# Two transformer layers on one core: a small matrix sent from another engine's DMA queue, and work of the query path, the token sums and the reloads put in other slots

## The chip, the core and the metric

The kernel runs on one core of a Trainium2 chip. The core has a matrix engine (TensorE; PE in the profile, PEld for its weight loads), three elementwise engines (VectorE: DVE, ScalarE: ACT, GpSimd: POOL), and SyncE (SP), which does nothing but issue DMAs. Sixteen DMA engines move data for all queues. The engines run on their own and meet through semaphores. The metric is the time of one execution in microseconds (us) on the device; lower is better.

## What is computed

Two layers over one sequence of 2048 tokens of width 448, in float32. With H = 16 heads of width 28 and F = 1792:

```python
phi = lambda t: jnp.where(t > 0, t + 1, jnp.exp(t)) + 1e-6
def A(x):                                  # linear attention
    q, k, v = split(x @ wqkv)              # (heads, tokens, 28) each
    pq, pk = phi(q), phi(k)
    kv = einsum("bhsd,bhse->bhde", pk, v); z = einsum("bhsd->bhd", pk)
    num = einsum("bhqd,bhde->bhqe", pq, kv)
    den = einsum("bhqd,bhd->bhq", pq, z) + 1e-6
    return (num / den) @ wo
def B(x):                                  # MLP
    return gelu(x @ w1 + b1) @ w2 + b2
for _ in range(2):
    x = x + A(layernorm(x))
    x = x + B(layernorm(x))
```

Each float32 matrix product is made of three passes: both operands are split into a high and a low part of a format that the matrix engine takes at full rate, and high by high, low by high and high by low are added up.

## The kernel before

The tokens stand in 16 tiles of 128, and in four blocks of 512. A layer has these stages. First come keys, values and queries of all tokens and the state of the attention; the queries go to DRAM (`pq_d`). Then a small transition forms from the state and `wo` a matrix M of 448 by 448, split into Mh and Ml, each in four pieces of 112 rows (`trans_ms`). Its use as weights (tiles `wq`) needs 128 rows to a tile, so `trans_chunks` (L916) copies rows between tiles by 14 DMAs, two to a chunk where a border falls inside; all are issued on SP's queue at L925, eight at the start of block 0 and six after the next piece of `mlp1`.

`classic(l, b, tr)` (L1321) then runs blocks 0 and 1 of the MLP, 14 steps each. In step i the matrix engine does `mlp1` of piece i+1 (11 matmuls into `hp`), what `behind` puts in, and `mlp2` of piece i (12 matmuls into four accumulators `y`). Between the two stands ScalarE's gelu (g, L1202) and its high part gh (L1173), and VectorE's low part gl (L1177). `make` prepares the next pair of pieces of w1: loads into `temp` (L420, L421, SP's queue) and casts into W (L425 and L430 on ScalarE, L426 to L432 on GpSimd).

`behind` (L1279) reads one row of the table `PLAN` for each of the 28 steps and does in it the query path of a later token tile, ahead of where the MLP needs it. For tile j of block k: `ld` loads pq (L942), `z` multiplies by the key sum (GpSimd, L952), `p` divides (VectorE: L963, L965, L967, L974) and transposes (L312, L313) into a square `sq`; `sq` stores this to DRAM (L319), and `lq` spreads it over the partitions (four DMAs at L331, tile `sp`); `q` splits that into qh (ScalarE, L365) and ql (VectorE, L366); `o` multiplies by wq (L1022 to L1026, into `op`), adds to x (L1043) and takes the norm's statistics; `n` and `sx`, `lx`, `x` do for the MLP's input what p, sq, lq, q do for the query. `r` and `b` load residuals and add the bias.

Blocks 2 and 3 share most of the MLP's first product by seven products in Strassen's manner: `eight(l, k)` (L1378), k = 0 to 6. Its operands are the four quarters A11, A12, A21, A22 of the tokens and the sums S1 to S4 of them (`token_sum`, L1107) split into high and low (`token_piece`: casts on ScalarE, L1112, subtractions on VectorE, L1113); the words s and t of PLAN make most of them in the last steps of block 1, `PLACES` gives each a slot. The weights of a product are sums of w1's pieces as well (VectorE, L458 to L480). The results of the products (hx, hy, hz) are read by copies and adds (L1146, L1401, L1418, L1423) and go through the gelu. Half of the gelus, those of block 3, go to DRAM (`g_d`), and `rest(l)` (L1454) brings them back (`gb`, loaded by `Came.load`, L1447), splits them and runs block 3's second product (w2 only). In between `rest` starts the next layer: x comes back (`load_to`, L86), is normalized (L528), transposed, stored (`sq_a`, L319), spread (`sp<-sq_a`, L331) and split (ScalarE, XH L365).

What sets the order: each engine runs its instructions in the order in which the program was written; nothing is rescheduled. All DMAs of SP and ScalarE take eight semaphores in turn, so an issue waits, whatever its data, until the DMA eight issues before it has landed. Tiles with one tag rotate through a fixed number of buffers ("e" has five; `gb` is of that tag), and a write into a buffer waits for the last reader of what it held.

Of the kernel before, what the change touches and what calls it, by code (L numbers as in the profile page):

```python
# [22 lines left out]
def linear_attn_mlp_kernel(  # L23
# [21 lines left out]
    G = 112  # L45
    NG = D // G
    NP = NF // 2
# [30 lines left out]
    def f(ap):  # L78
        return ap.bitcast(F32)
# [836 lines left out]
    def trans_chunks(tr):  # L916

        tr.ch = [(piece("q", c), piece("q", 3 + c)) for c in range(3)]
        tr.cr = piece("q", 6)

        def rows(src, out, at, lo, hi):
            r = lo
            while r < hi:
                n = min(hi, (r // G + 1) * G) - r
                sp.dma_start(f(out[at + r - lo:at + r - lo + n]), f(src[r // G][r % G:r % G + n]))  # L925
                r += n

        for c in range(3):
            if c == 2:
                yield  # L930
            rows(tr.Mh, tr.ch[c][0], 0, c * 128, (c + 1) * 128)
            rows(tr.Ml, tr.ch[c][1], 0, c * 128, (c + 1) * 128)
        rows(tr.Mh, tr.cr, 0, TL, D)
        rows(tr.Ml, tr.cr, 64, TL, D)


    pqt, qs, pzs = {}, {}, {}
# [114 lines left out]
    def add_bias(l, b, j):  # L1052
        t = b * 4 + j
        pool.tensor_tensor(xt[l, t], xt[l, t], b2b, op=OP.add)
# [12 lines left out]
    def m_prep(l, b, j):  # L1067
# [1 line left out]
        turn(xns.pop(("m", l, b * 4 + j)), ("m", l, b), j)  # L1069


    PLACES = ({"A11": 0, "S1": 1, "S2": 4, "A12": 5, "S3": 6, "S4": 2, "A22": 3},
              {"A11": 0, "S1": 5, "S2": 4, "A12": 1, "S3": 6, "S4": 2, "A22": 3})
    SUMS = {"S1": ("A21", "A22", OP.add), "S2": ("S1", "A11", OP.subtract),
            "S3": ("A11", "A21", OP.subtract), "S4": ("A12", "S2", OP.subtract)}
# [33 lines left out]
    def token_piece(l, name, h, eng=dve):  # L1109
        x = view(l, name, h)  # L1110
        hi, lo = (cols(placed(l, k, name, h)) for k in range(2))
        act.copy(hi, x)  # L1112
        eng.tensor_tensor(lo, x, f(hi), op=OP.subtract)  # L1113
# [91 lines left out]
    def mlp2(l, b, i, then=lambda: None):  # L1205
        gh, gl = gs.pop(i)
        first, last = i == 0, i == NF - 1
        n = i ^ (b > 1)
        hi, lo = w2h[:, n], w2l[:, n]
        end = l == LAYERS - 1 and b == NB - 1  # L1210
        if first:
            accs[l, b] = [bank("acc", 4, f"y{j}")[:, :D] for j in range(4)]
        acc = accs[l, b]
        for j in range(4):
            t = b * 4 + j
            s = slice(j * 128, (j + 1) * 128)
            if end and j == 3 and last:

                for h, eng in enumerate((act, sp)):
                    n = slice(h * D // 2, (h + 1) * D // 2)  # L1220
                    o = bank("m", 2, "yh")[:, :D // 2]
                    pe.matmul(o, gh[:, s], hi[:, n], start=True, stop=False)
                    pe.matmul(o, gh[:, s], lo[:, n], start=False, stop=False)
                    pe.matmul(o, gl[:, s], hi[:, n], start=False, stop=True)
                    xs = xt[l, t][:, n]
                    dve.tensor_tensor(xs, o, xs, op=OP.add)
                    eng.dma_start(x_d[l + 1][t * 128:(t + 1) * 128, n], xs)
                continue
            stop = last or (end and j == 3 and i == NF - 2)
            pe.matmul(acc[j], gh[:, s], hi, start=first, stop=False)  # L1230
            pe.matmul(acc[j], gh[:, s], lo, start=False, stop=False)  # L1231
            pe.matmul(acc[j], gl[:, s], hi, start=False, stop=stop)  # L1232
            if stop:
                xs = xt.pop((l, t)) if last else xt[l, t]
                dve.tensor_tensor(xs, acc[j], xs, op=OP.add)
                if j == 0:
                    then()
                if last:
                    sp.dma_start(x_d[l + 1][t * 128:(t + 1) * 128, :], xs)
# [7 lines left out]

    PLAN = (
        "p10 z11",
        "p11 sq10 z12 g10",  # L1250
        "p12 z13 lq10 g11",
        "p13 sq11 g12 g13 ld20",
        "q10 lq11 ld21",
        "q11 o10 ld22",
        "q12 o11 n10 ld23 z20",
        "q13 o12 n11 sx10 p20 z21",
        "o13 n12 lx10 p21 z22 sq20",
        "n13 sx11 p22 z23 lq20 g20 g21",
        "x10 lx11 p23 sq21 g22 g23",
        "x11 q20 lq21 ld30 ld31",  # L1260
        "x12 x13 q21 o20 ld32 ld33 z30",
        "q22 o21 n20 p30 z31",
        "q23 o22 n21 sx20 p31 z32 sq30",
        "o23 n22 p32 z33 lq30 g30 g31",
        "n23 sx21 p33 sq31 g32 g33",
        "q30 lq31 lx21 r10 r11",
        "q31 o30 r12 r13",
        "q32 o31 n30 tA111 b10",
        "q33 o32 n31 sx30 lx20 b11",
        "o33 n32 tA121 b12",  # L1270
        "n33 lx30 sx31 tA110 b13",
        "lx31 sS10 tA120",
        "tS10 sS30 sS20",
        "tS20 sS40 sS11 tS11 sS31",
        "tS40 sS21 tS21 sS41",
        "tA220 tA221 tS41",
    )

    def behind(l, i, tr):  # L1279
# [41 lines left out]
    def classic(l, b, tr):  # L1321

        if b == 0:
            mlp1(l, 0, 0)
            moves = trans_chunks(tr)
            next(moves)
        for i in range(NF):
            if i + 1 < NF:
                mlp1(l, b, i + 1)
            elif b == 0:  # L1330
                mlp1(l, 1, 0)
            if b == 0 and i == 0:
                next(moves, None)
            n = first_pair(l, b) + i // 2 + 2
            late = b and i >= NF - 4
            if late:
                if i > NF - 4:
                    make(first_pair(l, 2))
            elif i % 2:
                make(n)  # L1340
            if i % 2 == 0 and (b == 0 or i < NF - 2):
                make(n + 1)
            behind(l, b * NF + i, tr)
            if b == 0 and 9 <= i < 13:
                add_bias(l, 0, i - 9)
            if b == 0 or i < NF - 2:
                mlp2(l, b, i)
            if late:
                make(first_pair(l, 2))
            elif i % 2 == 0:  # L1350
                make(n)
            if b and i == NF - 1:
                make(n)

    def beside(l, k):

        nonlocal st_k, st_q
        if k == 0:
            for tok in "S30 S31".split():
                token_piece(l, tok[:-1], int(tok[-1]))  # L1360
        if 2 <= k < 6:
            back(l, 2, k - 2)
        if 3 <= k < 7:
            add_bias(l, 2, k - 3)
        if l + 1 == LAYERS:
            return
        if k == 6:
            load_to(l + 1, PRE - 1)
        if k == 1:
            st_k = stage_square(wqkv[:, D:2 * D])  # L1370
        if k == 2:
            split_kq("k", st_k)
        if k == 3:
            st_q = stage_square(wqkv[:, :D])
        if k == 4:
            split_kq("q", st_q)

    def eight(l, k):  # L1378

        n = first_pair(l, 2) + k  # L1380
        c = Pair(l, k, n)

        def step():
            if k < NP - 1:
                make(n + 1)

        c.product(1)
        s1 = c.keep(c.X, "s1")
        if k == 0:
            make(n)  # L1390
            beside(l, k)
        step()
        if k == 0:
            mlp2(l, 1, NF - 2)
            c.product(2)
            mlp2(l, 1, NF - 1)
        c.product(5)
        s5 = c.keep(c.Y, "s5")
        step()
        if k == 0:  # L1400
            dve.tensor_tensor(s1, s1, c.Z, op=OP.add)  # L1401
        if k:
            mlp2(l, 2, 2 * k - 1)
        c.product(6)
        s2 = c.keep(c.X, "s2")
        make(n)
        if k < NP - 2:
            make(n + 2)
        step()
        if k == 0:  # L1410
            c.high(s1, 0)
        else:
            c.product(2)
            dve.tensor_tensor(s1, s1, c.Z, op=OP.add)  # L1414
            c.high(s1, 0)
            step()
        c.product(7)
        dve.tensor_tensor(s5, c.X, s5, op=OP.add)  # L1418
        c.low(0)
        c.later(s5, 1)  # L1420
        step()
        c.product(3)
        dve.tensor_tensor(s2, s2, c.Y, op=OP.add)  # L1423
        c.high(s2, 1)
        step()
        c.product(4)
        if k == NP - 1:
            gb.load(l, 2)
        c.low(1)
        c.later(c.X, 0)  # L1430
        step()
        if k:
            beside(l, k)
        mlp2(l, 2, 2 * k)
        step()

    class Came:
# [5 lines left out]

        def load(self, l, n=1):
            for i in range(self.n, min(self.n + n, NF)):
                self.x[i] = t512("e", 5, "gb")
                sp.dma_start(self.x[i], g_d[l, i])  # L1447
            self.n = min(self.n + n, NF)

    gb = Came()  # L1450
# [136 lines left out]
```

## Time and profile before

| | |
|---|---|
| median of 3 runs | 892.22 us (891.28 to 892.72) |
| the profiled execution's own time | 889.03 us |
| its span, first to last instruction | 887.3 us |
| granted clock of the matrix engine, mean | 0.990 |
| matrix engine | 855.7 us busy, 4085 matmuls |
| DMA | 142.95 MB, mean 161 GB/s |

The profile is of one execution, so its stages add up to the span and not to the median; 1.7 us lie outside the span, and the execution is 3.2 us under the median. In rows of the timeline the columns are start, duration, engine, line, operation, output and inputs, and in brackets the idle time of the engine just ahead of the row, with what ended it. In rows of windows, each engine has its busy time and, in brackets, its count; PEclk is the granted clock as a share of full speed. Matmuls overlap: one that takes 0.36 us starts 0.20 us after the one before it, so starts are compared, not durations. Time that the matrix engine is idle is what there is to win; idle time of another engine counts only where the matrix engine waits for it.

### The profile page before, as it was taken

Reading aid. Unit: us, or ns where it says so; the run is one execution under the profiler, and the core shown is the slowest. Engines: PE = TensorE matmul, PEld = TensorE weight load, DVE = VectorE, ACT = ScalarE, POOL = GpSimd, SP = SyncE. Lnnn points to the kernel's source line nnn. Section 1 sums busy time; section 2 is a strip of 40 time slices with the busy share of each in tenths; the row PEclk is TensorE's granted clock in tenths of the full one; section 3 lists DMA queues with packets and bytes.
Section 4 is the critical chain, followed back from the end, with each engine's and each line's share of the span. In section 5 each row is a group of like instructions: output and inputs, shape, how many; then the busy total and the mean of one; then the engine's idle time right before and its main releaser. Section 6 shows DMA issues by size and latency. Waiting matters only on the chain.

```text
span 887.3 us, 12710 instructions
## 1 busy us (share of the span) xinstructions
PE 855.7 (96%) x4085; PEld 757.9 (85%) x4085; DVE 581.2 (65%) x1094; ACT 443.5 (50%) x883; POOL 384.3 (43%) x460
## 2 busy tenths in 40 slices
PE   9999999899999989999899999998999998899998
PEld 8999898688888868887699998987888887788887
DVE  7987686378976664456578876763879657534343
ACT  7667664334344557564345665543252435566531
POOL 3546533345644653650442243042556356444311
PEclk9999999899999999999999999998999999999999
DMA  5476746736576134316835543476375760332172
GB/s 172 139 240 197 197 137 209 224 120 217 202 240 203 48 119 138 126 66 233 235 117 178 183 136 94 145 223 211 129 229 198 241 196 23 118 109 89 48 233 83
DMA packets 105800, 142.95 MB, mean 161 GB/s; under 512 B 12036, under 2 KB 92804, under 8 KB 105732
## 3 DMA queue, kind: packets, MB, share of 16 engines
q1 hardware_dynamic: 104980, 141.72, 50.3%
q8 instruction: 32, 0.52, 0.3%
q10 hardware_dynamic: 752, 0.41, 0.2%
q14 instruction: 36, 0.29, 0.1%
HBM read 88.94 MB, written 49.02 MB: 155 GB/s over the span
## 4 chain that ended last, share of the span: by engine, by line
PE 72%; DMA 10%; DVE 9%; ACT 3%; issue 2%; SPq 2%; POOL 0%; DVEq 0%; ACTq 0%
PE hp L1200 10%; PE G L725 8%; PE psk L383 7%; PE psq L383 7%; PE hx L1142 7%; PE y L1230 7%; PE y L1231 6%; PE y L1232 6%; PE hy L1142 3%; DMA gb<-g_d 2%; DMA sp<-sq_m 2%; DMA sq_q<-sq 1%; DMA sp<-sq_q 1%; PE hz L1142 1%; DMA temp<-in_B_w_dram 1%
## 5 line engine op out<-in xcount | busy, mean ns | idle before, releaser
L1230 PE MATMUL y<-w2h,gh 128*128 128x448 f32 x447 | 164.0, 367 | 4.9 <-ACT gh L1173 3.8
L1231 PE MATMUL y<-w2l,gh 128*128 128x448 f32 x447 | 164.4, 368 | 0.0
L1232 PE MATMUL y<-w2h,gl 128*128 128x448 f32 x447 | 161.9, 362 | 1.3 <-DVE gl L1177 1.0
L1177 DVE TENSOR_TENSOR gl<-g,gh 128x512 fp32r<-128x512 f32 x84 | 64.3, 765 | 107.0 <-ACT gh L1173 107.0
L1200 PE MATMUL hp<-XH,W 128*128 128x512 f32 x392 | 123.3, 389 | 0.0
L1202 ACT ACTIVATE g<-hp,b1s 128x512 f32<-128x512 f32 x56 | 38.5, 688 | 159.5 <-PE hp L1200 159.5
L1230 PEld LDWEIGHTS y<-w2h,gh 128*128 128x128 f32 x447 | 84.5, 189 | 16.8 <-ACT gh L1173 5.6
L213 POOL TENSOR_TENSOR brs<-bve,few 128x1 f32<-128x1 f32 x55 | 35.4, 644 | 138.0 <-DVE bve L212 131.2
L1232 PEld LDWEIGHTS y<-w2h,gl 128*128 128x128 f32 x447 | 84.7, 189 | 9.6 <-DVE gl L1177 4.3
L1231 PEld LDWEIGHTS y<-w2l,gh 128*128 128x128 f32 x447 | 84.6, 189 | 6.4
L1200 PE MATMUL hp<-XL,W 128*128 128x512 f32 x224 | 85.2, 389 | 0.0
L1200 PEld LDWEIGHTS hp<-XH,W 128*128 128x128 f32 x392 | 73.5, 188 | 12.5
L383 PE MATMUL psk<-wk,XH 128*128 128x448 f32 x210 | 61.8, 364 | 0.0
L564 POOL TENSOR_TENSOR xnl<-x,xnh 128x384 fp32r<-128x384 f32 x32 | 35.3, 1103 | 60.3 <-PE psk L383 31.1
L426 POOL TENSOR_TENSOR W<-temp,W 128x256 fp32r<-128x256 f32 x56 | 46.1, 843 | 30.3 <-ACT W L425 30.2
L383 PE MATMUL psq<-wq,XH 128*128 128x448 f32 x196 | 57.0, 365 | 0.0
L1173 ACT CAST gh<-g 128x512 fp32r<-128x512 f32 x84 | 52.2, 621 | 2.7
L1154 ACT ACTIVATE g<-s,b1s 128x256 f32<-128x256 f32 x84 | 38.2, 502 | 29.9 <-DVE s L1414 14.8
L1200 PEld LDWEIGHTS hp<-XL,W 128*128 128x128 f32 x224 | 42.0, 188 | 8.8
L1142 PE MATMUL hx<-S,W 128*128 128x512 f32 x168 | 43.5, 392 | 4.5 <-DVE W L474 3.1
L725 PE MATMUL G<-kh,xnh 128*128 128x448 f32 x128 | 46.6, 367 | 0.0
L952 POOL TENSOR_TENSOR pz<-pq,zb 128x448 f32<-128x448 f32 x24 | 29.6, 1233 | 38.8 <-DMA pq<-pq_d 22.2
(249 smaller groups left out, 2024.6 us busy)
## 6 DMA issues: line engine op xcount, KB each, us to landing
temp<-in_B_w_dram SPq DMA_DIRECT2D x28, 384.0 KB
x<-in_A_x_dram SPq DMA_DIRECT2D x32, 224.0 KB
pq_d<-eq SPq DMA_DIRECT2D x32, 224.0 KB
pq<-pq_d SPq DMA_DIRECT2D x32, 224.0 KB
g_d<-g SPq DMA_DIRECT2D x28, 256.0 KB
gb<-g_d SPq DMA_DIRECT2D x28, 256.0 KB
x<-x_d SPq DMA_DIRECT2D x32, 224.0 KB
sq_a<-sq SPq DMA_DIRECT2D x13, 512.0 KB
```

The lines of the kernel that those rows point to most:

```text
L383: pe.matmul(o, x, p, start=(i == 0), stop=(i == 10))
L426: pool.tensor_tensor(lo, x, f(hi), op=OP.subtract)
L725: pe.matmul(acc[c], w, k, start=first and c not in others[0], stop=last and c not in others[1])
L1142: pe.matmul(o, w, r, start=(k in (1, 5, 2) and i == 0), stop=(i == len(made) - 1), skip_group_check=True)
L1154: act.activation(g[:, s].rearrange("p (u i n) -> p i u n", u=2, i=4), x[:, s].rearrange("p (i u n) -> p i u n", u=2, i=4), AF.Gelu_apprx_t ...
L1173: act.copy(gh, g)
L1177: dve.tensor_sub(gl, g, f(gh))
L1200: pe.matmul(hp, w, r, start=(k == 0), stop=(k == len(made) - 1))
L1202: act.activation(g, hp, AF.Gelu_apprx_tanh, bias=b1s[:, i:i + 1])
L1230: pe.matmul(acc[j], gh[:, s], hi, start=first, stop=False)
L1231: pe.matmul(acc[j], gh[:, s], lo, start=False, stop=False)
L1232: pe.matmul(acc[j], gl[:, s], hi, start=False, stop=stop)
```

## The change

The copies of `trans_chunks` are issued on ScalarE's queue in place of SP's, in seven pieces: the generator now stops after each half chunk, and `classic` calls it after `mlp1` and again after `mlp2` of each step of block 0 until it ends. The table PLAN gives the query steps p, sq, ld and z of blocks 2 and 3 to earlier or other steps, some token sums one step earlier, and makes the pieces of S3 in step 26 and none of A22. `PLACES` swaps the slots of S3 and A22 for the high parts. In `eight(l, 0)` the pieces of S3 are no longer made, and those of A22 come after product 6. At k = 5, in place of the end of k = 6, four gelus `gb` are loaded rather than two, and x of the next layer is loaded at k = 5 rather than 6. `gb` now uses the tags E and F as well, so that six are ahead rather than four.

```diff
@@ trans_chunks
-                sp.dma_start(f(out[at + r - lo:at + r - lo + n]), f(src[r // G][r % G:r % G + n]))
+                act.dma_start(f(out[at + r - lo:at + r - lo + n]), f(src[r // G][r % G:r % G + n]))
                 r += n
         for c in range(3):
-            if c == 2:
+            for src, k in ((tr.Mh, 0), (tr.Ml, 1)):
+                rows(src, tr.ch[c][k], 0, c * 128, (c + 1) * 128)
                 yield
-            rows(tr.Mh, tr.ch[c][0], 0, c * 128, (c + 1) * 128)
-            rows(tr.Ml, tr.ch[c][1], 0, c * 128, (c + 1) * 128)
         rows(tr.Mh, tr.cr, 0, TL, D)
         rows(tr.Ml, tr.cr, 64, TL, D)
+        yield
@@ PLACES
-    PLACES = ({"A11": 0, "S1": 1, "S2": 4, "A12": 5, "S3": 6, "S4": 2, "A22": 3},
+    PLACES = ({"A11": 0, "S1": 1, "S2": 4, "A12": 5, "S3": 3, "S4": 2, "A22": 6},
@@ PLAN
-        "q13 o12 n11 sx10 p20 z21",
+        "q13 o12 n11 sx10 ld32",
...
-        "tS20 sS40 sS11 tS11 sS31",
-        "tS40 sS21 tS21 sS41",
-        "tA220 tA221 tS41",
+        "sS40 tS20 sS11 sS31 tS11",
+        "sS21 tS21 sS41",
+        "tS30 tS31",
+        "tS40 tS41",
@@ classic
             moves = trans_chunks(tr)
-            next(moves)
...
-            if b == 0 and i == 0:
+            if b == 0:
                 next(moves, None)
...
                 mlp2(l, b, i)
+            if b == 0:
+                next(moves, None)
@@ beside
-        if k == 0:
-            for tok in "S30 S31".split():
-                token_piece(l, tok[:-1], int(tok[-1]))
...
+        if k == 5:
+            gb.load(l, 4)
         if l + 1 == LAYERS:
             return
-        if k == 6:
+        if k == 5:
             load_to(l + 1, PRE - 1)
@@ eight
             make(n)
-            beside(l, k)
...
         make(n)
+        if k == 0:
+            for h in range(2):
+                token_piece(l, "A22", h)
...
         c.product(4)
-        if k == NP - 1:
-            gb.load(l, 2)
@@ Came.load
-                self.x[i] = t512("e", 5, "gb")
+                tag = "EEFFeeee"[i % 8]
+                self.x[i] = t512(tag, 5 if tag == "e" else 2, "gb")
```

SP's queue at the start of block 0 of layer 0, before; L925 are the copies into wq, `temp` are pieces of w1, `sq_q_1_0` is the first query square of block 1, stored, and then spread at L331:

```order
L925 DMA wq_1729<-Ml 80x448
L925 DMA wq_1729<-Ml 48x448
L925 DMA wq_1730<-Mh 64x448
L925 DMA wq_1730<-Ml 64x448
L420 DMA temp<-in_B_w_dram 128x3x256
L421 DMA temp<-in_B_w_dram 128x1x256
L319 DMA sq_q_1_0_1825<-sq 128x1024
L86 DMA x_4_1829<-in_A_x_dram 128x448
L420 DMA temp<-in_B_w_dram 128x3x256
L421 DMA temp<-in_B_w_dram 128x1x256
L331 DMA sp<-sq_q_1_0_1825 32x4x256 x4
```

The same place after the change, from the last store of queries (L688) on; `pq_8` is the query tile that `ld20` loads:

```order
L688 DMA pq_d_71<-eq 128x448
L420 DMA temp<-in_B_w_dram 128x3x256
L421 DMA temp<-in_B_w_dram 128x1x256
L942 DMA pq_8_1809<-pq_d_71 128x448
L319 DMA sq_q_1_0_1819<-sq 128x1024
L86 DMA x_4_1823<-in_A_x_dram 128x448
L420 DMA temp<-in_B_w_dram 128x3x256
L421 DMA temp<-in_B_w_dram 128x1x256
L331 DMA sp<-sq_q_1_0_1819 32x4x256 x4
```

The 14 copies are gone from here, so the first pair of temp follows the store of queries, and one load of pq stands ahead of the store of the square.

ScalarE's queue in steps 1 to 3 of block 0, before: casts of w1 and a gelu with its high part in turn.

```order
L430 CAST W_130<-temp 128x512
L1202 ACTIVATE g<-hp,b1s 128x512
L1173 CAST gh<-g 128x512
L425 CAST W_130<-temp 128x2x128 x2
L1202 ACTIVATE g<-hp,b1s 128x512
L1173 CAST gh<-g 128x512
```

And after the change, the same casts and gelus:

```order
L430 CAST W_130<-temp 128x512
L925 DMA wq_1745<-Ml 96x448
L925 DMA wq_1745<-Ml 32x448
L1202 ACTIVATE g<-hp,b1s 128x512
L1173 CAST gh<-g 128x512
L925 DMA wq_1746<-Mh 80x448
L925 DMA wq_1746<-Mh 48x448
L925 DMA wq_1747<-Ml 80x448
L925 DMA wq_1747<-Ml 48x448
L425 CAST W_130<-temp 128x2x128 x2
L1202 ACTIVATE g<-hp,b1s 128x512
L1173 CAST gh<-g 128x512
```

The issues now stand between the casts and gelus, and each of these waits until the issues ahead of it are done.

VectorE at the entry of `eight(0, 0)`, before, from the last piece of S2 to the low part of S3; L467 and L474 are weight sums, L1107 a token sum, the XL are low parts of A22 and of S4's second half:

```order
L1113 TENSOR_TENSOR S_3314<-sp,S_3313 128x2x256
L1107 TENSOR_TENSOR sp<-sp 128x2x4x64
L467 TENSOR_TENSOR W_130<-raw,W_130 128x512
L1113 TENSOR_TENSOR XL<-sp,XH 128x2x256 x3
L474 TENSOR_TENSOR W_130<-raw,W_130 128x256
L475 TENSOR_TENSOR W_130<-raw,W_130 128x128
L1113 TENSOR_TENSOR S_3389<-sp,S_3388 128x2x256 x2
```

After the change, in two pieces. The first is the entry, from the last gl of block 1 on, the second a few rows on, around the add that was L1418 and is now L1420:

```order
L1177 TENSOR_TENSOR gl<-g,gh 128x512
L1113 TENSOR_TENSOR S_3361<-sp,XH 128x2x256 x2
L467 TENSOR_TENSOR W_130<-raw,W_130 128x512
L1113 TENSOR_TENSOR XL<-sp,XH 128x2x256 x2
L474 TENSOR_TENSOR W_130<-raw,W_130 128x256
```

```order
L1235 TENSOR_TENSOR r_7_2997<-y_2708,r_7_2997 128x448
L1400 TENSOR_TENSOR s_3386<-s_3386,hz 128x512
L480 TENSOR_TENSOR W_130<-raw,W_130 64x128
L1113 TENSOR_TENSOR XL<-sp,A_3452 128x2x256 x2
L1420 TENSOR_TENSOR s_3437<-hx,s_3437 128x512
```

Two token sums (L1107) and a low part have left the entry, the pieces of S3 stand ahead of L467, and two subtractions, those of A22, stand right ahead of the add.

More of the change, by code (lines that the diff above doesn't have):

```diff
@@ L1249, in linear_attn_mlp_kernel @@
         "p10 z11",
[L1250 to L1255, printed above, removed]
-        "q13 o12 n11 sx10 p20 z21",
[L1257 to L1272, printed above, removed]
+        "p11 sq10 z12 g10 ld20",
+        "p12 z13 lq10 g11 ld21",
+        "p13 sq11 z20 g12 g13 ld22",
+        "q10 lq11 p20 z21 ld23",
+        "q11 o10 p21 sq20 z22 ld30",
+        "q12 o11 n10 p22 z23 ld31",
+        "q13 o12 n11 sx10 ld32",
+        "o13 n12 lx10 p23 sq21 z30",
+        "n13 sx11 p30 z31 g20 ld33",
+        "x10 lx11 lq20 p31 sq30 z32 g21",
+        "x11 q20 lq21 p32 z33 g22",
+        "x12 x13 q21 o20 p33 sq31 g23",
+        "q22 o21 n20 lq30 g30",
+        "q23 o22 n21 sx20 g31",
+        "q30 o23 n22 lq31 g32 g33",
+        "q31 o30 n23 sx21",
+        "q32 o31 n30 r10 r11",
+        "q33 o32 n31 sx30 lx21 r12 r13",
+        "o33 n32 lx20 tA111 b10",
+        "n33 sx31 lx30 tA121 b11",
+        "tA110 b12",
+        "lx31 sS10 tA120 b13",
         "tS10 sS30 sS20",
-        "tS20 sS40 sS11 tS11 sS31",
-        "tS40 sS21 tS21 sS41",
-        "tA220 tA221 tS41",
+        "sS40 tS20 sS11 sS31 tS11",
+        "sS21 tS21 sS41",
+        "tS30 tS31",
+        "tS40 tS41",
     )
```

## The prediction

> **What bounds the kernel now.** The page's first part is read first, then the waits of the matrix engine.
>
> ```profile
> PE 855.7 (96%) x4085; PEld 757.9 (85%) x4085; DVE 581.2 (65%) x1094; ACT 443.5 (50%) x883; POOL 384.3 (43%) x460
> ```
>
> ```profile
> PE op L1022 <- DMA x<-in_A_x_dram: 4.4, 1, 4.4
> PE op L1022 <- ACT qh L365: 3.9, 1, 3.9
> PE y L1230 <- ACT gh L1173: 3.8, 4, 1.4
> PE hx L1142 <- DVE s L1418: 3.7, 2, 1.8
> PE hx L1142 <- DVE W L474: 3.1, 2, 1.6
> PE hy L1142 <- DVE W L467: 1.6, 2, 0.8
> PE op L1024 <- DVE ql L366: 1.6, 2, 0.8
> PE hx L1142 <- ACT s L1146: 1.4, 2, 0.7
> ...
> PE y L1232 <- DVE gl L1177: 1.0, 1, 1.0
> PE y L1230 <- DVE x L1235: 0.9, 2, 0.5
> ```
>
> The matrix engine is busy 855.7 of 887.3 us, and the change takes no matmul away, so nearly all that it can win is these waits (total, times, longest), and what the clock loses behind them. They lie at four places: the first use of wq in each layer (op L1022, 8.3 us), two short ones of the query path (op L1024 and y L1230 behind x, 2.5), the entry of `eight` (hx and hy, 9.8), and `rest` of layer 0 (y behind gh and gl, 4.8). The change touches all four.
>
> **The first use of wq.** The timeline and the windows of layer 0, and a window of layer 1:
>
> ```profile
> 167.28 0.74 PE L1022 MATMUL op<-wq,qh 128*128 128x448 f32 x1 [4.36 <-DMA x<-in_A_x_dram]
> 172.58 0.37 PE L1230 MATMUL y<-w2h,gh 128*128 128x448 f32 x1
> 172.79 0.36 PE L1231 MATMUL y<-w2l,gh 128*128 128x448 f32 x1
> ```
>
> ```profile
> 165.60:172.50 6.90, 5.22 (x14) 4.52 (x15) 2.92 (x5) 3.48 (x7) 3.41 (x4) 0.51 0.83 229
> 600.00:622.00 22.00, 18.07 (x77) 15.66 (x76) 7.69 (x15) 6.30 (x13) 4.82 (x7) 0.84 0.70 218
> ```
>
> Behind 4.36 us of idleness 14 matmuls ran at a clock of 0.51: they took 172.58 − 167.28 = 5.3 us, and 14 starts 0.2 us apart would be 2.8, so the clock cost 2.5 more. In layer 1 the mean clock of 0.84 over 22 us is 7 us at half, as long a stretch, so I take 2.5 there too. Together 4.4 + 2.5 + 3.9 + 2.5 = 13.3 us. What ended the wait is read from the other engines:
>
> ```profile
> 149.07 0.27 DVE L313 STREAM_TRANSPOSE sq<-pq 128x128 f32<-128x128 f32 x1
> ```
>
> ```profile
> 150.14 0.59 SPq L925 DMA_DIRECT2D wq<-Ml  x1
> ...
> 152.11 0.40 SPq L319 DMA_DIRECT2D sq_q<-sq  x1
> ...
> 159.24 1.77 SPq L331 DMA_DIRECT2D sp<-sq_q  x4
> ```
>
> ```profile
> 166.60 0.62 ACT L365 CAST qh<-sp 128x512 fp32r<-128x512 f32 x1 [6.70 <-DMA sp<-sq_q]
> ```
>
> The square is complete in SBUF at 149.34, yet its store is issued at 152.11, because the copies (about 0.6 us each on SP) and a pair of temp stand ahead of it. The spread follows 7.13 us later, and qh 7.36 us after that. So the wait named after x is one for the spread of the square.
>
> *After.* The 14 issues leave SP's queue, and the pair of temp goes out ahead of this stretch, so the store is issued at about 149.5, when its data are there: 2.6 us earlier. If store and spread then take as long as now (14.5 us in all), qh starts at 164.0 rather than 166.6 and 1.8 us of the wait remain. They should be faster: two pairs of temp (512 KB each) lie around the store now, and one will. At the 229 GB/s of the window one pair is 2.2 us; against it stand the later copies, which now run beside the store on ScalarE's queue. Bounds for both layers: −5.2 us (2.6 each, half clock as before) and −13.3. I take −12, nearer to the second, since 1.8 us are left at worst to one pair's 2.2.
>
> [...]
>
> **ScalarE's price.** The four steps that take the copies, with ScalarE's busy time alone, and a wait of SP:
>
> ```profile
> 139.20:158.80 19.60, 7.16 (x14) 1.00 0.71 225
> ```
>
> ```profile
> SPq L925 <- DMA temp<-in_B_w_dram: 4.4, 3, 2.5
> ```
>
> 14 issues of 0.6 us are 8.4 us, with 7.16 of casts and gelus 15.6 of 19.6: 4.0 us to spare, 1 per step. The copies waited for landings on SP too (the second row: the DMA eight issues before is a piece of temp), and on ScalarE the gelu behind would wait with them, and then `mlp2`, and the matrix engine. Bounds 0 and +3 per layer; I take +0.5 per layer, +1, because the pair of temp in question is now issued some 11 us before the copy that waits for it.
>
> **The two short waits of the query path.**
>
> ```profile
> 205.00:219.00 14.00, 13.22 (x63) 11.45 (x62) 11.38 (x17) 7.23 (x15) 7.45 (x7) 1.00 0.74 236
> ```
>
> VectorE is busy 11.38 of 14 us around the wait for ql; the new PLAN takes the division and transposes of block 2's later tiles out of these steps. It puts them in steps 4 to 9, where VectorE has less room than today. All gone is −2.5 and the refill of the pipeline, −3.5; a like number of new waits in the fuller steps is +3. I take −2, as the steps that empty are those with a wait in the trace.
>
> **The entry of eight.** Its window, then VectorE, then the matrix engine there:
>
> ```profile
> 309.40:320.00 10.60, 6.47 (x25) 4.42 (x26) 9.96 (x17) 6.04 (x14) 6.93 (x8) 1.00 0.29 98
> ```
>
> ```profile
> 304.39 1.22 DVE L1177 TENSOR_TENSOR gl<-g,gh 128x512 fp32r<-128x512 f32 x1
> ...
> 308.72 0.69 DVE L467 TENSOR_TENSOR W<-raw,W 128x512 fp32r<-128x512 f32 x1
> ...
> 311.68 0.94 DVE L474 TENSOR_TENSOR W<-raw,W 128x256 fp32r<-128x256 f32 x1
> ...
> 313.00 1.82 DVE L1113 TENSOR_TENSOR S<-sp,S 128x512 fp32r<-128x512 f32 x2
> ...
> 318.64 0.69 DVE L1418 TENSOR_TENSOR s<-hx,s 128x512 f32<-128x512 f32 x1
> ```
>
> ```profile
> 309.46 0.50 PE L1142 MATMUL hy<-XH,W 128*128 128x512 f32 x1 [0.80 <-DVE W L467]
> ...
> 312.67 1.43 PE L1142 MATMUL hx<-S,W 128*128 128x512 f32 x5 [1.56 <-DVE W L474]
> ...
> 319.38 0.73 PE L1142 MATMUL hx<-XH,W 128*128 128x512 f32 x2 [1.83 <-DVE s L1418]
> ```
>
> VectorE is full (9.96 of 10.6) and each wait is for the next row of its queue. After the change two token sums and a low part (0.7 each) leave the stretch between gl and L467, and two pieces of S3 (1.8, the row at 313.00) come ahead of L467. Starting from today's gl, which ends at 305.6, or 2 us earlier if the gl is no longer held up by sums ahead of it (the sums are a step earlier), L467 ends 0.7 + 1.8 us behind it, at 306 to 308.1. The matrix engine would want it at 309.46 − 0.80 = 308.7: gone. Two low parts (0.8 each) and L474 (0.94) follow, to 308.6 to 310.7, wanted at 312.67 − 0.80 − 1.56 = 310.3: gone or 0.4 left. From the end of L474 (312.62) to the add (318.64) are 6.0 us today, 4.2 without S3's pieces; with those of A22 (1.6) and the add itself (0.7) it ends at 315.1 to 317.2. Wanted at 319.38 less the 4.2 us of waits for VectorE: 315.2. So 0 to 2 us remain of 4.2. The 0.7 for ScalarE's copy of s stays, as its order there stays. Bounds for two layers −4 and −10 (with refills); I take −7.5, near the middle.
>
> **Rest of layer 0.**
>
> ```profile
> 392.00:405.00 13.00, 13.00 (x62) 11.23 (x61) 4.73 (x9) 8.21 (x20) 1.76 (x2) 1.00 0.24 69
> 405.00:442.00 37.00, 32.31 (x141) 26.45 (x140) 23.50 (x49) 12.04 (x23) 10.46 (x12) 0.95 0.84 266
> ```
>
> ```profile
> 435.30:438.70 3.40, 3.00 (x8) 2.70 (x9) 2.49 (x4) 0.00 (x0) 1.14 (x1) 0.50 0.95 252
> ```
>
> ```profile
> 434.06 0.47 PE L1230 MATMUL y<-w2h,gh 128*128 128x448 f32 x1 [1.35 <-ACT gh L1173]
> ...
> 435.70 0.74 PE L1232 MATMUL y<-w2h,gl 128*128 128x448 f32 x1 [0.97 <-DVE gl L1177]
> ...
> 440.28 0.47 PE L1230 MATMUL y<-w2h,gh 128*128 128x448 f32 x1 [0.92 <-ACT gh L1173]
> ```
>
> ```profile
> 439.09 0.62 ACT L365 CAST XH<-sp 128x512 fp32r<-128x512 f32 x1 [5.09 <-DMA sp<-sq_a]
> ```
>
> Idle time is 37.00 − 32.31 = 4.7 us, and 3.4 us at half clock lose 1.7 more: 6.4. The DMAs move 266 GB/s here and 69 in the 13 us before. Four gelus of 256 KB and five tiles of x of 224 KB, 2.1 MB, now leave one product earlier, which is 8 us of transfers at 266 GB/s out of the crowded stretch, though part of it was issued before 405 already. The waits for gb should go. What is late next: ScalarE splits x of the next layer (XH, 439.09) ahead of the cast of the gelu that ends the wait at 440.28. With no waits those matmuls would start some 6 us earlier, at 434, and the spread would have to land 6 us earlier as well. Bounds 0 (the spread is where it was, and one wait takes all) and −7; I take −4.5, as 8 us of transfers are more than the 6 that are wanted, but not all were in the way.
>
> **Sum.** −12 + 1 − 2 − 7.5 − 4.5 = −25 us against the profiled execution's 889.03: 864. That execution is 3.2 us under the median, so 867.2, say **867**. The ends of all terms together give −34 (858) and about 0 (892).
>
> **Rivals.**
>
> *The spread stays late.* Only SP's issue time is saved, and the copies crowd the same DMA engines beside the store. For it: the DMA share is 0.83 in the window above, so an earlier issue may only queue longer. Against it: the pair of temp that stood ahead of the store is away. The gain at wq is 5.2 instead of 12: 874; with the half clock kept and little won in `rest`, 879. [...]
>
> *New waits take the place.* Steps 4 to 9 overfill VectorE (+3), ScalarE's issues cost 3 per layer (+6), and A22's pieces keep the add late: 885 to 891.
>
> *ScalarE held, on the other side.* An issue on ScalarE waits for a landing while a gelu stands behind it. It decides where such holds exceed the 4.0 us to spare in the four steps. Two waits of 4 us in each layer, with the clock's 2.5 behind each as in the row at 167.28, cost 4 × 6.5 = 26, and the copies land too late to win anything at wq: +26 − 2 − 7.5 − 4.5 = +12, 904. For it speaks SP's row of waits for temp; against it that these were 2.5 us at the longest, on a queue that issued them back to back, where ScalarE spreads them over four steps.
>
> *It all goes.* Every wait above, refills and half clock: under 859.
>
> **How the numbers follow.** Chances: the forecast with its terms between 859 and 874, 0.63; the spread late, 874 to 882, 0.14; new waits, 882 to 892, 0.10; slower, by ScalarE or a wait like it, 0.09; under 859, 0.04. The range 859 to 882 holds 0.77, and to 883 with the lower part of the new waits about 0.8. A measurement of this kernel can tell about 0.2% (1.8 us) from no change. New waits within that of 892 get 0.04. So faster 0.87, same 0.04, slower 0.09.
>
> **What would show it.** In the changed profile the store L319 should be issued by 150 and qh L365 start by 162 to 164, with no stretch at a clock of 0.5 behind op L1022; that row shrinks from 4.4 and 3.9 to under 2 each. Rows of hx and hy for W should vanish, and one for the add (now L1420) remain under 2 us each. In `rest` a row of y for gh should remain, ended by XH's spread and not by gb. Wrong would be: a wait of y for gh in block 0's steps 2 to 5 (ScalarE held), a low clock that stays behind op L1022, or new waits for ql or x in steps 4 to 9.

## The result, and the profile after

The changed kernel takes 879.31 us (median of 4 runs, 878.12 to 880.39), the kernel before on the same chip 891.99 (4 runs): a ratio of 0.9857, 95% interval 0.984 to 0.9875. That is 12.7 us less, half of the 25 that the terms of the prediction add up to. The profiled execution took 878.12 us, its span 876.4, against 889.03 and 887.3 before: 10.9 us less. The page's first line and the waits of the matrix engine after the change:

```profile
PE 852.0 (97%) x4085; PEld 757.7 (86%) x4085; DVE 577.1 (66%) x1094; ACT 443.1 (51%) x883; POOL 384.6 (44%) x460
```

```profile
PE op L1022 <- ACT qh L365: 9.3, 4, 3.7
PE y L1230 <- ACT gh L1173: 5.4, 2, 5.2
PE hx L1142 <- DVE s L1420: 2.3, 2, 1.1
PE hx L1142 <- ACT s L1146: 1.4, 2, 0.7
```

The rows for W, for ql and for x are gone, as forecast, and the add's row is under 2 us each. But op L1022 waits for qh four times rather than twice and longer in total than before (9.3 us to 8.3), and one wait of y for gh is 5.2 us long.

To sum up a place I take each matmul's start less the start of the one before it, less the usual distance for its kind; this counts idle time, half clock and the refill of the pipeline together (behind a wait at full clock the first matmul starts 0.31 us ahead of the second, rather than 0.20: op L1024 at 214.23 before). By place, in us, of the two profiled executions:

| place | lost before | lost after | forecast | measured |
|---|---|---|---|---|
| first use of wq, with ScalarE's price (both layers) | 13.6 | 4.9 | −11 | −8.8 |
| query path, later steps (both) | 3.6 | 11.2 | −2 | +7.5 |
| entry of eight (both) | 11.9 | 4.7 | −7.5 | −7.3 |
| rest (both) | 10.5 | 8.2 | −4.5 (layer 0 alone) | −2.3 |
| sum | | | −25 | −10.9 |

The sum agrees with the difference of the two spans, 887.3 − 876.4, so nothing of size lies outside these four places. The forecast has 14.1 us more than was measured: 9.5 of them went in the second row, 2.2 each in the first and the fourth. The forecast of the fourth row was for layer 0 alone, and there the loss fell by only 0.9 us (9.1 to 8.2); the other 1.4 are two short waits of layer 1's `rest` that went.

**The new wait.** The timeline of the matrix engine, of ScalarE and of SP in layer 0, step 12 of the table, after the change:

```profile
211.84 0.47 PE L1022 MATMUL op<-wq,qh 128*128 128x448 f32 x1 [3.05 <-ACT qh L365]
```

```profile
211.17 0.62 ACT L365 CAST qh<-sp 128x512 fp32r<-128x512 f32 x1 [4.85 <-DMA sp<-sq_q]
```

```profile
198.86 0.42 SPq L420 DMA_DIRECT2D temp<-in_B_w_dram  x1
199.33 0.53 SPq L421 DMA_DIRECT2D temp<-in_B_w_dram  x1
201.75 1.77 SPq L331 DMA_DIRECT2D sp<-sq_m  x4
203.56 4.84 SPq L331 DMA_DIRECT2D sp<-sq_q  x4
```

This is the first query tile of block 2 (o20). Its spread, `lq20`, stands in step 10, behind the spread of a square of the MLP's input (`lx11`) and a pair of temp; its four issues take 4.84 us, as the last waits until 208.10 for the landing of the temp issued at 199.33, and they are over only at 208.4. Before the change lq20 stood in step 9 and its row read:

```profile
202.88 1.74 SPq L331 DMA_DIRECT2D sp<-sq_q  x4
```

That was ahead of the other spread and of the temp, and the issues were not held. The windows around it after the change:

```profile
209.20:212.60 3.40, 0.70 (x3) 0.34 (x3) 0.78 (x2) 1.40 (x3) 0.28 (x1) 1.00 0.92 281
212.60:216.10 3.50, 3.50 (x10) 3.11 (x11) 3.36 (x7) 2.60 (x6) 2.63 (x2) 0.51 1.07 269
```

Half clock follows the wait, so the place loses 5.3 us in layer 0, and 5.9 in layer 1 at 648.

**The wait in rest.** ScalarE and SP in `rest` of layer 0, after the change:

```profile
423.25 0.62 ACT L1173 CAST gh<-gb 128x512 fp32r<-128x512 f32 x1 [1.31 <-PE y L1231]
432.31 0.62 ACT L365 CAST XH<-sp 128x512 fp32r<-128x512 f32 x1 [8.44 <-DMA sp<-sq_a]
432.83 0.61 ACT L1173 CAST gh<-gb 128x512 fp32r<-128x512 f32 x1
```

```profile
414.24 0.60 SPq L1448 DMA_DIRECT2D gb<-g_d  x1
...
421.44 5.11 SPq L331 DMA_DIRECT2D sp<-sq_a  x4
```

The gelu that is cast at 432.83 was asked for at 414.24 and landed at 421.30, and its cast waits for nothing of its own; it stands behind the split of x, which waits 8.44 us for its spread. The waits for gb are gone, and the split that the prediction named as late next is late.

### The profile page after: what moved, and what is told of

The parts are those of the page before. It is cut to its first block, busy times and chain, and to the rows that moved or that the text cites. A ratio compares the mean times of both kernels' runs of the same rounds, so it can differ in the third digit from the quotient of the medians.

```text
span 876.4 us, 12701 instructions
## 1 busy us (share of the span) xinstructions
PE 852.0 (97%) x4085; PEld 757.7 (86%) x4085; DVE 577.1 (66%) x1094; ACT 443.1 (51%) x883; POOL 384.6 (44%) x460
## 4 chain that ended last, share of the span: by engine, by line
PE 77%; DMA 10%; DVE 5%; ACT 3%; issue 2%; POOL 1%; SPq 1%; ACTq 0%; DVEq 0%; POOLq 0%
PE hp L1200 9%; PE G L725 8%; PE psk L383 8%; PE y L1231 8%; PE y L1230 7%; PE y L1232 7%; PE hx L1142 7%; PE psq L383 6%; DMA temp<-in_B_w_dram 4%; PE hy L1142 3%; PE op L1024 2%; PE op L1023 2%; PE op L1022 2%; DMA sp<-sq_q 2%; PE hz L1142 1%
## 5 line engine op out<-in xcount | busy, mean ns | idle before, releaser
L1177 DVE TENSOR_TENSOR gl<-g,gh 128x512 fp32r<-128x512 f32 x84 | 67.9, 808 | 103.1 <-ACT gh L1173 103.1
L426 POOL TENSOR_TENSOR W<-temp,W 128x256 fp32r<-128x256 f32 x56 | 48.7, 889 | 12.4 <-ACT W L425 12.4
L1154 ACT ACTIVATE g<-s,b1s 128x256 f32<-128x256 f32 x84 | 38.2, 502 | 27.6 <-DVE s L1416 14.1
L725 PE MATMUL G<-kl,xnh 128*128 128x448 f32 x128 | 46.0, 365 | 0.0
```

The source lines that it names most:

```text
L426: pool.tensor_tensor(lo, x, f(hi), op=OP.subtract)
L725: pe.matmul(acc[c], w, k, start=first and c not in others[0], stop=last and c not in others[1])
L1154: act.activation(g[:, s].rearrange("p (u i n) -> p i u n", u=2, i=4), x[:, s].rearrange("p (i u n) -> p i u n", u=2, i=4), AF.Gelu_apprx_t ...
L1177: dve.tensor_sub(gl, g, f(gh))
```

## The experiments

Each is timed against the kernel before on its own chip.

**The spread a step earlier.** One word of PLAN in the changed kernel:

```diff
-        "n13 sx11 p30 z31 g20 ld33",
-        "x10 lx11 lq20 p31 sq30 z32 g21",
+        "n13 sx11 lq20 p30 z31 g20 ld33",
+        "x10 lx11 p31 sq30 z32 g21",
```

> The changed kernel with one word of PLAN moved: lq20, the spread of block 2's first query square, stands in step 9 ahead of the other spreads instead of in step 10 behind lx11. The square has been in DRAM since 178.7 us, so nothing but its place holds the spread. Theory (the new wait of op L1022 at 211.8 and 647.9 is this spread, issued behind four others and a pair of temp): both waits and the half clock behind them go, 5.3 + 5.9 = 11 us less than the changed kernel, about 868 us and a ratio to the kernel before of 0.973. Rival (the DMA engines are full there, so the spread lands at 211 wherever it is issued, or another wait takes its place at once): within 2 us of the changed kernel, 877 to 881.

Measured 867.7 us, ratio 0.9746 (0.9706 to 0.9787), where the changed kernel has 0.9857. Its row of the waits, and SP's queue there:

```profile
PE op L1022 <- ACT qh L365: 3.6, 2, 1.8
```

```profile
196.04 2.57 SPq L331 DMA_DIRECT2D sp<-sq_q  x4
```

Two of the four waits are left, those of the first use of wq; both new ones are gone, with no half clock near. The DMA engines had room: the spread is issued 7.5 us earlier, and no other wait comes up at this place. Of the 11 us won here, 1.7 are lost again in `rest`, where the one long wait grows from 5.2 to 6.1 us.

**The same place, in the kernel before.** The opposite move:

```diff
-        "n13 sx11 p22 z23 lq20 g20 g21",
-        "x10 lx11 p23 sq21 g22 g23",
+        "n13 sx11 p22 z23 g20 g21",
+        "x10 lx11 lq20 p23 sq21 g22 g23",
```

> The kernel before with one word of PLAN moved the other way: lq20 in step 10 behind lx11 instead of step 9. Theory (this place alone makes the wait): a new wait of op L1022 for qh of 3 to 5 us in both layers near 211 and 651, with half clock behind it, 8 to 12 us slower than before, about 900 us, ratio 1.01. Rival (the wait in the changed kernel came from the other moves, more query work ahead of it): within 2 us of the kernel before.

Measured 900.15 us, ratio 1.0112 (1.0072 to 1.0152). The wait appears, with the half clock behind it (0.50 from 216.50 to 219.90, after 3.40 us without a matmul):

```profile
216.79 0.74 PE L1022 MATMUL op<-wq,qh 128*128 128x448 f32 x1 [3.79 <-ACT qh L365]
```

So this place in the table suffices to make the wait; the rest of the new query order is not needed for it.

**The split of x later.** One table of `rest` in the changed kernel:

```diff
-    REST = ("a0", "n0 a1", "n1", "s0 a2 m0", "n2 a3 m1", "n3", "s1 m0 p0", "a4 m0", "n4 x0", "x1 m1", "p1", "m1", "x2", "x3")
+    REST = ("a0", "n0 a1", "n1", "s0 a2 m0", "n2 a3 m1", "n3", "s1 m0 p0", "a4 m0", "n4", "m1", "p1", "x0 m1", "x1 x2", "x3")
```

> The changed kernel with one row of the table of rest moved: the split of the next layer's first tiles of x (x0) stands two steps later, behind the casts of two more reloaded gelus; x1 follows it. Theory (what holds the matrix engine at 433.5 is the cast of a gelu that landed at 421.3 but stands on ScalarE behind the split, which waits for its spread until 432.3): the 5.2 us wait and the half clock go, 6 to 7.5 us less than the changed kernel, about 872 us, and no row of y for gh over 1.5 us in layer 0's rest. Rival (the reloads themselves are late): the wait shrinks by less than 2 us, since the next cast then waits for its own data, or the wait moves to the first product of layer 1, and the time stays at 877 or above.

Measured 873.58 us, ratio 0.9809 (0.9774 to 0.9845); the profiled execution's span is 868.6, 7.8 us under that of the changed kernel. In its waits there is no row of y for gh. The window of `rest`, of the changed kernel first and then of this one:

```profile
403.00:440.00 37.00, 31.75 (x144) 27.96 (x143) 23.22 (x48) 10.66 (x20) 15.64 (x16) 0.91 0.65 205
```

```profile
403.00:440.00 37.00, 36.93 (x184) 34.00 (x183) 27.66 (x54) 13.15 (x26) 18.13 (x18) 1.00 0.66 205
```

184 matmuls instead of 144 in the same time at the same DMA rate. In the changed kernel the transfers were not what bound `rest`; ScalarE's order was. By the two ratios the gain is about 4 us (0.9857 to 0.9809, with intervals that just overlap), by the profiles 7.8; the stage itself lost 8.2 us before the move and 0.6 after it.

**The copies alone**, in the kernel before:

```diff
-                sp.dma_start(f(out[at + r - lo:at + r - lo + n]), f(src[r // G][r % G:r % G + n]))
+                act.dma_start(f(out[at + r - lo:at + r - lo + n]), f(src[r // G][r % G:r % G + n]))
...
+            for src, k in ((tr.Mh, 0), (tr.Ml, 1)):
+                rows(src, tr.ch[c][k], 0, c * 128, (c + 1) * 128)
                 yield
...
-            if b == 0 and i == 0:
+            if b == 0:
                 next(moves, None)
```

> The kernel before with the copies into wq alone changed: seven pieces on ScalarE's queue, everything else as before. Theory (the copies out of SP's queue are worth what the stage shows, 13.6 us lost before and 4.7 after): 8 to 10 us less than before, about 883 us, ratio 0.990, with waits of op L1022 of 1 to 2 us per layer and no half clock there; the other places as before. Rival (the early load and the query steps moved by PLAN are needed for it): 3 us or less.

Measured 885.49 us, ratio 0.996 (0.993 to 0.999): 3.6 us by the ratio, and not the 8 to 10. The stage did win that: the two waits of op L1022 went from 8.3 to 3.7 us without half clock, and the place lost 4.9 us rather than 13.6. But 4.9 of the 8.7 came back in its profile further on: 1.7 at the entry of eight in layer 1, 1.9 in the query path, 1.3 in `rest`. The ten executions of this kernel lie between 883.66 and 893.66 us, so how much comes back may differ from one to the next. At that entry the waits for W are those of before, but the clock halves behind them; two windows of the kernel with the copies alone, and one of the kernel before:

```profile
751.70:755.10 3.40, 1.56 (x7) 0.99 (x6) 2.75 (x6) 2.15 (x5) 1.23 (x2) 1.00 0.93 320
755.10:758.50 3.40, 3.40 (x10) 2.96 (x9) 1.78 (x4) 2.22 (x6) 0.00 (x0) 0.50 0.51 156
```

```profile
309.00:312.40 3.40, 1.65 (x6) 1.05 (x6) 3.40 (x5) 2.07 (x5) 2.15 (x2) 1.00 0.08 22
```

With 1.56 us of matmuls in 3.4 the clock halved in the next stretch, with 1.65 (before) it did not. The theory had the stage right and the total wrong.

**The copies back on SP's queue**, in the changed kernel, at the same seven places of the program:

```diff
-                act.dma_start(f(out[at + r - lo:at + r - lo + n]), f(src[r // G][r % G:r % G + n]))
+                sp.dma_start(f(out[at + r - lo:at + r - lo + n]), f(src[r // G][r % G:r % G + n]))
```

> The changed kernel with the seven pieces issued on SP's queue at the same places of the program. Theory (what counts is that the copies are spread over four steps, and the eight semaphores tie both queues anyway): within 2 us of the changed kernel, 877 to 881. Rival (the queue counts: on SP a copy that waits for a landing holds the store of the square and the pieces of temp behind it): the wait of op L1022 at 165 and 600 grows by 2 us or more each and may bring the half clock back, 882 to 890.

Measured 877.76 us, ratio 0.9855 (0.9828 to 0.9883), the same as the changed kernel. So the other queue is not what helps. What this run and the one before it leave is that the copies no longer stand as one block ahead of the store. Counted as in the table, the first use of wq even loses less on SP's queue, 2.8 us against 4.9, but the times don't tell the two apart.

**Both repairs together**, lq20 in step 9 and the split of x later.

> The changed kernel with both moves together: lq20 in step 9, and the split of x in rest two steps later. Theory (two separate waits, each put where it is by one late spread): the gains add, 10 and 6 us less than the changed kernel, 861 to 864 us, ratio about 0.967. Rival (the half clock or a later wait gives part back, as the copies alone gave back half of theirs): 865 or more.

Measured 861.6 us, ratio 0.9685 (0.9641 to 0.9729). The gains add. In the profiled execution the half clock is back at the first use of wq in layer 0, behind a wait of 1.67 us:

```profile
162.70:166.10 3.40, 1.68 (x7) 0.86 (x6) 1.22 (x2) 1.86 (x5) 0.00 (x0) 1.00 0.94 298
166.10:169.50 3.40, 3.40 (x10) 2.98 (x10) 3.28 (x6) 1.62 (x3) 3.26 (x4) 0.50 0.98 322
```

The place loses 4.5 us there, where the changed kernel's profile has 2.6 after a wait of 1.19. So the wait that is left can still bring the half clock. Of the four executions two have a mean clock of 1.000 and two of 0.998 and 0.996.

**Both repairs, and the copies on SP's queue.**

> The same with the copies into wq issued on SP's queue in the same seven places. Theory (the queue does not matter, their spread over four steps does): within 2 us of the version with ScalarE's queue; the wait for gh at 153 goes (0.8 us) and the waits of op L1022 at 165 and 600 are no longer. Rival (ScalarE's queue is worth something once the other waits are gone): 2 us or more slower than that version.

Measured 860.7 us (860.02 to 861.82), ratio 0.9667 (0.9639 to 0.9695). Against the version on ScalarE's queue this is no difference that the intervals allow; in the profile the mean clock is 1.000, with

```profile
PE op L1022 <- ACT qh L365: 1.2, 2, 0.6
```

for the first use of wq, where the other has 3.5 us; but 1.4 us of waits for ql (op L1024) stand behind them at the same place, which the other hasn't. Both versions are about 2% under the changed kernel by the ratios, and this one has the lowest median of all.

**The reloads alone**, in the kernel before:

```diff
+        if k == 5:
+            gb.load(l, 4)
...
-        if k == 6:
+        if k == 5:
             load_to(l + 1, PRE - 1)
...
-        if k == NP - 1:
-            gb.load(l, 2)
...
-                self.x[i] = t512("e", 5, "gb")
+                tag = "EEFFeeee"[i % 8]
+                self.x[i] = t512(tag, 5 if tag == "e" else 2, "gb")
```

> The kernel before with the part on rest alone: four gelus and x loaded one product earlier, gb in the tags E and F, six ahead. Theory (the loads come early enough, but the split of x stays ahead of a cast on ScalarE and takes the wait over): the waits for gb at 414 go, one long wait for gh with half clock stays near 440, 1 to 3 us less than before, ratio 0.997 to 0.999. Rival (the loads bound rest by themselves, and only lost their gain to other parts of the change): 6 us or more less than before, ratio 0.993 or under.

Measured 887.59 us, ratio 0.9961 (0.9943 to 0.998). The waits at 414 are gone and one is left:

```profile
PE y L1230 <- ACT gh L1173: 5.8, 1, 5.8
```

with the split ahead of the cast again (ScalarE is idle for 8.92 us until the spread for XH has landed). The interval holds the theory's 0.997, the point lies a little under it, and the rival's 0.993 is out.

**The split later alone**, in the kernel before, the same edit of REST.

> The kernel before with the split of x in rest two steps later and nothing else. Theory (in the kernel before too, the split holds the cast that ends the wait at 440.28, but the earlier waits at 414 and 434 are for the reloads): the wait at 440 goes and the half clock of layer 0's rest stays or moves, 1 to 3 us less than before, ratio 0.997 to 0.999. Rival (the split is all of it): 6 us or more less.

Measured 888.57 us, ratio 0.9962 (0.9943 to 0.998). Two waits for gh are left, at 415 and 435, and one of 1.0 us for gl at 437:

```profile
PE y L1230 <- ACT gh L1173: 2.9, 2, 1.6
```

Alone each of the two edits is worth 3 to 4 us by the ratios, with a wait left that goes when both are made. Their profiles don't show where: counted as in the table, `rest` loses 9.7 us with the reloads alone and 10.1 with the split alone, against 10.5 before.

**The entry alone**, in the kernel before: the slots of PLACES as in the change, and

```diff
-        "tS20 sS40 sS11 tS11 sS31",
-        "tS40 sS21 tS21 sS41",
-        "tA220 tA221 tS41",
+        "sS40 tS20 sS11 sS31 tS11",
+        "sS21 tS21 sS41",
+        "tS30 tS31",
+        "tS40 tS41",
...
-            for tok in "S30 S31".split():
-                token_piece(l, tok[:-1], int(tok[-1]))
...
+            for h in range(2):
+                token_piece(l, "A22", h)
```

> The kernel before with the entry of eight alone changed: the last four rows of PLAN, the slots of S3 and A22, the pieces of S3 in step 26 and those of A22 after product 6. Theory (the term is what the stage shows, 12 us lost there before and 4.7 after, and stands on its own): the rows of hx and hy for W go, one of hx for the add of 1 to 1.4 us stays, 6 to 8 us less than before, ratio 0.992. Rival (part of it is given back later, as with the copies alone, where short waits further on met a window that halved the clock): 3 to 5 us less, with more stretches of half clock than before.

Measured 888.52 us, ratio 0.9977 (0.9961 to 0.9993), a smaller gain than the theory's and the rival's. In its profile the entry lost 8.5 us instead of 11.9, and a row for W is still there, which the changed kernel hasn't:

```profile
312.17 1.42 PE L1142 MATMUL hx<-S,W 128*128 128x512 f32 x5 [0.97 <-DVE W L474]
```

So the new pieces alone win half of the 7.3 us; the other half belongs to the rest of the change, most likely to the query work and sums that end a step earlier and leave VectorE free. That is not shown: which rows of the table do so was not tried.

## Why the prediction was right or wrong

The time lies in the range and the sign is right; the likeliest value was 12 us too low. That 879 is in the range is in part luck. The upper part, from 874 on, stood for a spread that stays late at the first use of wq, and that did not happen; what filled it was a wait at a place where the prediction saw a gain.

*The first use of wq.* The mechanism holds. The store of the square goes out earlier and the half clock behind op L1022 is gone:

```profile
149.00 0.32 SPq L319 DMA_DIRECT2D sq_q<-sq  x1
...
154.65 0.53 SPq L421 DMA_DIRECT2D temp<-in_B_w_dram  x1
155.23 3.02 SPq L331 DMA_DIRECT2D sp<-sq_q  x4
```

```profile
164.40 0.62 ACT L365 CAST qh<-sp 128x512 fp32r<-128x512 f32 x1 [4.03 <-DMA sp<-sq_q]
```

The store is issued at 149.00, against the 149.5 that was forecast, but qh starts at 164.40 and not by 162 to 164. Between the store and the first spread it takes 6.23 us, against 7.13 before; from there to qh it takes 9.17, against 7.36, so the time is lost behind the start of the spread. The issue of temp at 154.65 waited for a copy's landing (154.64), and the last of the four spreads, at 157.94, for another (157.92): the copies are on ScalarE's queue, but they are in the same round of eight semaphores. The term was mis-sized, −12 against −9.8 (ScalarE's price apart), in part by these waits of SP's queue for the copies. The half clock is gone from this profile, but the run with both repairs shows that it can come back.

*ScalarE's price* was forecast at +1. A gelu was held by a copy that waited for the landing of temp at 151.51, and the matrix engine lost 0.8 us at 153.5 in layer 0 and 0.3 at the same place of layer 1. It went no further, though that temp took 11.7 us to land; the prediction had counted on 11.

```profile
151.53 0.52 ACTq L925 DMA_DIRECT2D wq<-Ml  x1
152.11 0.69 ACT L1202 ACTIVATE g<-hp,b1s 128x512 f32<-128x512 f32 x1 [2.05 <-PE hp L1200]
```

```profile
153.50 0.47 PE L1230 MATMUL y<-w2h,gh 128*128 128x448 f32 x1 [0.18 <-ACT gh L1173]
```

*The query path* is the step that failed. The prediction said "I take −2, as the steps that empty are those with a wait in the trace", and put the danger into VectorE's load in steps 4 to 9. The two short waits did go. But the steps were read for VectorE's work and not for the DMAs that they issue on SP's queue: lq20 had moved from step 9 to step 10, one step ahead of its use, behind four other spreads and a pair of temp. The bound of +3 was for VectorE; the place lost 7.5 us more than before. Moving that word back took all of it away (0.9857 to 0.9746), and moving it in the kernel before put the wait there.

*The entry* came out at −7.3 against −7.5. The steps of the sum were near too: L467 was to end between 306 and 308.1 and ended at 305.8, and of the 4.2 us of waits for VectorE 1.1 stayed, all for the add behind A22's pieces:

```profile
305.08 0.68 DVE L467 TENSOR_TENSOR W<-raw,W 128x512 fp32r<-128x512 f32 x1
```

```profile
314.85 0.70 PE L1142 MATMUL hx<-A,W 128*128 128x512 f32 x2 [1.13 <-DVE s L1420]
```

That the sum depends on the rest of the table was not seen; the entry's edits alone win half.

*Rest* named what would be late next, and sized it wrongly. It counted on the 8 us of transfers moved ahead to bring the spread of x early enough. The spread landed 6.8 us earlier (XH at 432.31 instead of 439.09), but the matrix engine also came to its wait earlier, at 428, by all that had been won before, so the wait was longer (5.2 us) and halved the clock for 6.8 us. The term was for layer 0, where −0.9 was measured against −4.5; that lies within its bounds, but near the end at which one wait takes all. Of the waits before, the one of 1.35 us, to 434.06, stood ahead of the half clock, which began at 435.30, and of the one of 0.97, from 434.73 to 435.70, only a part did.

*Rivals.* "New waits take the place" came nearest, in kind but not in place. "The spread stays late" is half right: putting the copies back on SP changed nothing, but the gain at wq was 9.8 us and not 5.2, since the order on the queue changed and not the queue alone. The times don't tell the two queues apart (ratios 0.9855 on SP's and 0.9857 on ScalarE's). ScalarE held for long, and all waits gone, did not happen.

## What to carry to other kernels

A table that moves steps moves their DMAs as well: for every step that changes its place, look at what stands ahead of its transfers on their queue and how many steps are left until they are used; one step was too few here, two enough. A cast that waits for a transfer belongs behind the casts whose data are already there, since an engine in order makes all of them wait (ScalarE was idle for 8.44 us here ahead of the split, and the gelu that it cast next, at 432.83, had landed at 421.30). A part of a change, timed alone, can show less than its stage has won, because the matrix engine then comes earlier to the next late transfer and waits longer there; sum up the losses by place before and after.

## What the runs showed of the hardware

The clock can halve without a whole idle stretch. In the records of the two profiles, before and after, it changes at steps of 3.41 us whose beginning differs from run to run, and a stretch at half lasts 3.41 or 6.83 us. Apart from the end of each it fell at 165.65, 435.30 and 605.97 before and at 212.63, 431.08 and 649.54 after; in the 3.41 us ahead of these falls the matrix engine was busy for 0.68, 1.49, 1.33, 0.73, 0.65 and 1.59 us. Behind four steps at full clock with 1.65, 1.71 and 1.66 us (from 309.01, 315.84 and 749.33 before) and 1.50 (from 642.71 after) it did not fall. In the rows of the other runs 1.56 and 1.68 of 3.40 us were followed by half clock. So no sharp line shows, but a step that is busy for about half can be enough. Two short waits that fall into one such step can then cost 1.7 us more, an estimate from half of 3.41, in the next execution perhaps not, as the beginning of the steps moves. With the copies alone the entry of layer 1 lost 7.6 us so, against 6.0 before. But half clock is not always a loss: in the same run it stood at the entry of layer 0 too (0.50 from 311.40 to 314.80, behind 1.44 us of matmuls in 3.40), and from the matmul that waits for L467 to the one that waits for the add it took 9.92 us (306.34 to 316.26), as before (309.46 to 319.38); the wait for the add was 0.37 us instead of 1.83.

Copies issued on two engines were not independent. In the profiles before and after, the 677 issues take eight semaphores in turn, each 84 or 85 times; an issue on SP waited for the landing of a copy of ScalarE's (154.65, landing at 154.64) and the other way round. Held so for over 0.2 us were 17 issues before, all on SP, and 37 after, 16 of them across the two queues; each began 0.02 us behind the landing of the DMA that had used its semaphore last. And the landing of one small piece of w1 (128 KB) took up to 11.7 us in the crowded stretch, so that the issue eight places later could not go before that (ScalarE's at 151.53, behind the landing at 151.51).

The matmuls on split parts are the fastest by column in these two profiles: at full clock they start 0.20 us apart for 448 columns and 0.23 for 512. A product of whole operands (L901, 448 columns) stands in two records that start 0.375 us apart.
